# K and V tails with zero rows for the other pair of heads, in a fused attention and expert kernel

## The chip, the cores and the metric

The kernel runs on one core of one Trainium2 chip. The metric is device time in microseconds (us) of one execution; the figure for a kernel is the median of several executions. A second source of numbers is one execution that the hardware profiler recorded, instruction by instruction; its own time and span stand beside the median below.

## The reference

Three blocks follow each other: a linear attention with a norm per head, a feed-forward block with squared ReLU, and a mixture of four experts. Only the first is touched.

```python
def _attn_ref(q, k, v, g_norm):          # 4 batches, 8 heads, 576 positions, 64 wide
    kv = np.einsum('bhsd,bhse->bhde', k, v)
    out = np.einsum('bhsd,bhde->bhse', q, kv)
    rms = np.sqrt(np.mean(out * out, axis=-1, keepdims=True) + 1e-06)
    return out / rms * g_norm
def _moe_ref(x, w_in, w_out):            # 2304 tokens, 512 -> 2048 -> 512
    h = np.maximum(x @ w_in, 0.0)
    return h * h @ w_out
def _moe2_ref(x, domain_probs, w1, w2):  # 4 experts, 512 -> 1024 -> 512, weighted by probs
    ...
```

## The kernel before

**Attention.** Two heads are put side by side, so that a pair is 128 columns wide; there are 4 batches with 4 pairs each, 16 pairs in all. For pair i, `att_kv(i)` (lines 451 to 462) sums K-transposed times V over the 576 positions into one PSUM tile `pk`: four matmuls over 128 positions each (line 457, operands `kvs` or `kvm`), and one over the last 64 positions, the tail (line 458, operand `kvt`). The two diagonal 64x64 blocks of `pk` are copied to `kvd`, one by ScalarE (line 460) and one by VectorE (line 461). `att_out(t)` multiplies a tile of 128 positions of q with four of the `kvd` blocks (line 472, into `po`); ScalarE squares it (line 481), VectorE sums the squares (line 482). `att_c` makes the norm's factor for a group of tiles on VectorE and writes the normed tile `xn` (line 504). `att_b` transposes `xn` on TensorE (line 515, into `pt`), and ScalarE and GpSimd split the result into a high and a low part `x` (lines 213 and 214). All of attention is done in float32, and the trace shows two records for each such matmul.

**The tail.** `kvt[b]` holds the tails of a batch's four pairs on 128 partitions: pairs 0 and 2 on partitions 0 to 63, pairs 1 and 3 on partitions 64 to 127. The tail matmul of a pair reads its 64 partitions only; the trace gives its shape as 64x128, that of line 457 as 128x128.

**Order.** `RAMP` is a list of units (k: `att_kv`, o: `att_out`, c: `att_c`, b: `att_b`, w and y: narrowing and splitting of weights, f and g: first and second matmul of the feed-forward block). The units of the ramp go through a scheduler that sets the order of each engine's instructions from its own estimates of their times; only the second stage, the experts, is in an order written out by hand. Every engine runs its own instructions in order and waits for others by semaphores. Nearly all loads go through the queue of SyncE (SP), also in order. `load_kv(i + 8)` is called at the end of `att_kv(i)` (line 462), `load_q(t + 4)` in `att_out(t)` (line 479). The tiles `kvm` (pairs 6 to 15) and `kvt` have two buffers, `q` has four, so that a load may have to wait until TensorE has read what lay there: the load of `kvm9` waits for the line 457 matmuls of pair 7.

**After attention**, TensorE runs the matmuls of the feed-forward block (lines 550, 564, 723) and of the experts (lines 845 and 909) until the end. Their weights come in as `raw` (line 234), are narrowed by ScalarE and VectorE (lines 240 to 257) and split by ScalarE and GpSimd (lines 394 to 396).

Of the kernel before, what the change touches and what calls it, by code (L numbers as in the profile page):

```python
# [10 lines left out]
F32 = mybir.dt.float32  # L11
# [7 lines left out]
P = 128  # L19
B, H, S, D = 4, 8, 576, 64  # L20
# [3 lines left out]
STAIL = S - NCK * P  # L24
# [158 lines left out]
def fused_kernel(ctx, tc, kvm, kvt, qt, g2, probs, probs_t, w64, w32, out, out_t):  # L183
    nc = tc.nc
# [241 lines left out]
    kv_in, q_in, tails, stage, st_t, po_t, att_mid = {}, {}, {}, [None], {}, {}, {}  # L426
    NSTAGE = 6

    def load_kv(i):
        if i >= B * NPAIR:  # L430
            return
        b, c = divmod(i, NPAIR)
        if i < NSTAGE:
            if i % 2 == 0:
                stage[0] = accp.tile([P, 2, 2, NCK, P], F32, tag=f"acc{i // 2 + 1}", name=f"kvs{i}")
            m = stage[0][:, i % 2]
        else:
            m = attp.tile([P, 2, NCK, P], F32, tag="kvm", name=f"kvm{i}")
        nc.sync.dma_start(out=m, in_=kvm[b, c])
        if c == 0:  # L440
            tails[b] = attp.tile([P, 2, 2, P], F32, tag="kvt", name=f"kvt{b}")
            nc.sync.dma_start(out=tails[b], in_=kvt[b])
        kv_in[i] = m

# [6 lines left out]
    def att_kv(i):  # L451
        m = kv_in.pop(i)
        b, c = divmod(i, NPAIR)
        tl = tails[b][c % 2 * STAIL : (c % 2 + 1) * STAIL, c // 2]
        pk = ps.tile([P, 512], F32, tag="ps", name=f"pk{i}")
        for n in range(NCK):
            nc.tensor.matmul(pk[:, :P], m[:, 0, n, :], m[:, 1, n, :], start=(n == 0), stop=False)  # L457
        nc.tensor.matmul(pk[:, :P], tl[:, 0, :], tl[:, 1, :], start=False, stop=True)
        kd = kvd[i % NKVD]
        nc.scalar.activation(out=kd[:D, :D], in_=pk[:D, :D], func=AF.Copy)  # L460
        nc.vector.tensor_copy(kd[D:, D:], pk[D:, D : 2 * D])
        load_kv(i + NSTAGE + 2)
# [472 lines left out]
    def probs_keep():  # L935
# [10 lines left out]

    unit = dict(
        k=att_kv, o=att_a, c=att_c, b=att_b, w=split_w, y=split_narrowed, p=probs_p, n=probs_keep, f=g1, g=g2a, x=right, e=right_first, l=half_load, s=g1s, h=g2b, q=g2q, r=second_right, u=prepare, d=move
    )
    ext = early = None  # L950
# [4 lines left out]
    with ExitStack() as actx:  # L955
        attp = actx.enter_context(tc.tile_pool(name="attp", bufs=2))
# [12 lines left out]
        for _ in range(2):  # L969
            nc.tensor.matmul(idle, zero[:, :P], zero, start=True, stop=True)  # L970
        nc.scalar.activation(out=warm, in_=warm, func=AF.Sqrt)
        load_kv(0)
        load_kv(1)
        load_w(0)
        load_kv(2)
# [69 lines left out]
```

## Time and profile before

| | us |
|---|---|
| median of 3 runs | 1157.28 (1157.25 to 1157.65) |
| the profiled execution, its time | 1157.0 |
| the profiled execution, its span | 1155.1 |
| TensorE busy (share of the span) | 1138.3 (99%) |
| VectorE, GpSimd, ScalarE busy | 927.6, 786.3, 514.8 |
| tail matmuls on TensorE | 16 instructions, 32 records |

The span runs from the first to the last instruction, and the execution's time lies 1.9 us above it. Of the views, two matter most here. The chain of waits follows the work that ended last back from the last instruction; each of its rows is a start, a length and what filled it, so that consecutive records of one kind show TensorE's pace. The timeline lists the instructions of an engine in order of time, with the idle time before each and what ended it.

### The profile page before, as it was taken

Reading aid. Unit: us, or ns where it says so; the run is one execution under the profiler, and the core shown is the slowest. Engines: PE = TensorE matmul, PEld = TensorE weight load, DVE = VectorE, ACT = ScalarE, POOL = GpSimd, SP = SyncE. Lnnn points to the kernel's source line nnn. Section 1 sums busy time; section 2 is a strip of 40 time slices with the busy share of each in tenths; the row PEclk is TensorE's granted clock in tenths of the full one; section 3 lists DMA queues with packets and bytes.
Section 4 is the critical chain, followed back from the end, with each engine's and each line's share of the span. In section 5 each row is a group of like instructions: output and inputs, shape, how many; then the busy total and the mean of one; then the engine's idle time right before and its main releaser. Section 6 shows DMA issues by size and latency. Waiting matters only on the chain.

```text
span 1155.1 us, 15647 instructions
## 1 busy us (share of the span) xinstructions
PE 1138.3 (99%) x5514; PEld 953.2 (83%) x5514; DVE 927.6 (80%) x1471; ACT 514.8 (45%) x897; POOL 786.3 (68%) x675
## 2 busy tenths in 40 slices
PE   8999999999999999999999999999999999999998
PEld 6878888888888887888888888888778888888886
DVE  6866789788676667888888888888978888888888
ACT  4575545555444564644445444445543221212121
POOL 2566666656464666888888888878876565656565
PEclk9999999999999999999999999999999999999999
DMA  8811130855464535888778888875665646565652
GB/s 310 283 46 55 56 146 19 310 179 206 146 214 160 191 92 186 309 256 276 247 246 283 265 255 255 264 264 139 162 193 190 256 160 264 167 247 194 235 184 89
DMA packets 62549, 231.03 MB, mean 200 GB/s; under 512 B 6115, under 2 KB 20195, under 8 KB 46215
## 3 DMA queue, kind: packets, MB, share of 16 engines
q1 hardware_dynamic: 56278, 210.20, 50.2%
q0 software_dynamic: 5760, 19.66, 9.1%
q8 instruction: 44, 0.72, 0.2%
q14 instruction: 35, 0.28, 0.1%
q10 hardware_dynamic: 432, 0.17, 0.1%
HBM read 138.49 MB, written 71.86 MB: 182 GB/s over the span
## 4 chain that ended last, share of the span: by engine, by line
PE 93%; POOL 2%; DMA 2%; ACT 1%; DVE 1%; issue 1%; SPq 0%; DVEq 0%; POOLq 0%; ACTq 0%
PE p L564 17%; PE p L550 10%; PE pc L723 10%; PE pa L723 10%; PE pd L723 10%; PE qc L845 7%; PE qd L845 7%; PE qa L845 7%; PE pb L723 5%; PE qb L845 4%; PE p L909 4%; PE po L472 1%; DMA kvs<-in_kvm 1%; PE pk L457 1%; DMA raw<-in_w 1%; DMA b<-hb 1%
## 5 line engine op out<-in xcount | busy, mean ns | idle before, releaser
L564 PE MATMUL p<-hh,b 128*128 128x512 f32 (+1 forms) x640 | 193.8, 369 | 0.0
L214 POOL TENSOR_TENSOR hl<-r,hh 128x512 fp32r<-128x512 f32 (+1 forms) x80 | 98.4, 1242 | 91.3 <-ACT hh L213 91.2
L564 PEld LDWEIGHTS p<-hh,b 128*128 128x128 f32 x640 | 116.8, 189 | 20.2 <-ACT hh L213 0.2
L214 POOL TENSOR_TENSOR b<-hb,b 128x512 fp32r<-128x512 f32 x62 | 81.1, 1309 | 69.9 <-ACT b L213 69.8
L571 DVE TENSOR_TENSOR acc<-p,acc 128x512 f32<-128x512 f32 (+1 forms) x140 | 87.7, 634 | 40.8 <-PE p L564 39.6
L564 PE MATMUL p<-hl,b 128*128 128x512 f32 (+1 forms) x320 | 118.3, 370 | 0.8 <-POOL hl L214 0.8
L213 ACT ACTIVATE b<-hb 128x512 fp32r<-128x512 f32 x62 | 38.9, 627 | 169.4 <-PE qa L845 159.9
L214 POOL TENSOR_TENSOR a<-w,a 128x512 fp32r<-128x512 f32 x44 | 62.2, 1419 | 56.7 <-ACT a L213 56.7
L723 PE MATMUL pa<-o,a 128*128 128x512 f32 x384 | 98.1, 391 | 2.2 <-ACT p L734 2.2
L723 PE MATMUL pc<-o,a 128*128 128x512 f32 x384 | 97.6, 389 | 0.8 <-DVE u L738 0.8
L723 PE MATMUL pd<-o,a 128*128 128x512 f32 x384 | 97.7, 390 | 0.1
L723 PEld LDWEIGHTS pc<-o,a 128*128 128x128 f32 x384 | 72.0, 188 | 16.2 <-DVE u L738 1.3
L723 PEld LDWEIGHTS pa<-o,a 128*128 128x128 f32 x384 | 71.0, 188 | 17.0 <-ACT p L734 3.1
L723 PEld LDWEIGHTS pd<-o,a 128*128 128x128 f32 x384 | 71.9, 188 | 15.6 <-DVE pb L743 0.8
L550 PE MATMUL p<-x,a 128*128 128x512 f32 (+1 forms) x432 | 83.8, 344 | 0.1
L550 PEld LDWEIGHTS p<-x,a 128*128 128x128 f32 x432 | 69.4, 189 | 11.0 <-POOL x L214 0.6
L564 PEld LDWEIGHTS p<-hl,b 128*128 128x128 f32 x320 | 60.4, 189 | 11.5 <-POOL hl L214 1.6
L867 DVE TENSOR_TENSOR acct<-qc,acct 128x512 f32<-128x512 f32 x90 | 61.8, 686 | 2.5 <-POOL acct L875 2.1
L867 DVE TENSOR_TENSOR acct<-qa,acct 128x512 f32<-128x512 f32 x90 | 61.5, 685 | 0.2 <-PE qa L845 0.2
L845 PE MATMUL qd<-t4b,b 128*128 128x512 f32 x192 | 54.5, 391 | 1.3 <-DVE acct_r L867 0.8
L214 POOL TENSOR_TENSOR t<-t1f,t 128x512 fp32r<-128x512 f32 x31 | 45.4, 1463 | 14.1 <-ACT t L213 14.1
L845 PE MATMUL qa<-t4b,b 128*128 128x512 f32 x192 | 54.1, 390 | 0.6 <-POOL t4b L214 0.6
(230 smaller groups left out, 2952.4 us busy)
## 6 DMA issues: line engine op xcount, KB each, us to landing
raw<-in_w SPq DMA_DIRECT2D x64, 512.0 KB, 4.6
a_kept<-a SPq DMA_DIRECT2D x28, 1024.0 KB, 4.8
a<-a_kept SPq DMA_DIRECT2D x28, 1024.0 KB, 10.2
t<-th_kept_t SPq DMA_DIRECT2D x27, 1024.0 KB, 6.9
b_kept<-b SPq DMA_DIRECT2D x14, 1024.0 KB, 6.2
bs<-bs_kept SPq DMA_DIRECT2D x14, 1024.0 KB, 7.3
b<-raw POOLq DMA_DIRECT2D x16, 512.0 KB, 5.1
bs_kept<-o SPq DMA_DIRECT2D x7, 1024.0 KB, 4.3
```

The lines of the kernel that those rows point to most:

```text
L213: nc.scalar.activation(out=hi, in_=full, func=AF.Copy)
L214: engine.tensor_tensor(out=lo, in0=full, in1=hi.bitcast(F32), op=ALU.subtract)
L457: nc.tensor.matmul(pk[:, :P], m[:, 0, n, :], m[:, 1, n, :], start=(n == 0), stop=False)
L472: nc.tensor.matmul(po[done : done + n, c * P : (c + 1) * P], q[:, c, done : done + n], kvd[(b * NPAIR + c) % NKVD], start=True, stop=True,)
L550: nc.tensor.matmul(pt[:, :n], w, x, start=(i == 0), stop=(i == len(steps) - 1))
L564: nc.tensor.matmul(pt[:, :n], w, h, start=(i == 0), stop=(i == len(steps) - 1))
L571: nc.vector.tensor_tensor(out=a, in0=pt[:, :n], in1=a, op=ALU.add)
L723: nc.tensor.matmul(pr[bank], x, y, start=(m == 0 and not more), stop=(m == len(steps) - 1), skip_group_check=more,)
L845: nc.tensor.matmul(pt, x, y, start=(m == 0 and not more), stop=(m == len(steps) - 1), skip_group_check=more)
L867: nc.vector.tensor_tensor(out=to, in0=pt, in1=to, op=ALU.add)
L909: nc.tensor.matmul(pt, h, w, start=(i == 0), stop=(i == len(steps) - 1))
```

## The change

The host lays the tails out anew. For each pair of neighbours (0 and 1, 2 and 3) the tile has three blocks of 128 columns on 128 partitions: K of the even pair with zeros on partitions 64 to 127, V of both, K of the odd pair with zeros on partitions 0 to 63. The tail matmul now takes all 128 partitions, with K from the first or the third block and V from the second; the zeros cancel the other pair's rows. The load of a batch's tails grows from 256 KB to 384 KB.

```diff
         if c == 0:
-            tails[b] = attp.tile([P, 2, 2, P], F32, tag="kvt", name=f"kvt{b}")
+            tails[b] = attp.tile([P, 2, 3, P], F32, tag="kvt", name=f"kvt{b}")
             nc.sync.dma_start(out=tails[b], in_=kvt[b])
...
-        tl = tails[b][c % 2 * STAIL : (c % 2 + 1) * STAIL, c // 2]
+        tl = tails[b][:, c // 2]
...
-        nc.tensor.matmul(pk[:, :P], tl[:, 0, :], tl[:, 1, :], start=False, stop=True)
+        nc.tensor.matmul(pk[:, :P], tl[:, c % 2 * 2, :], tl[:, 1, :], start=False, stop=True)
...
-    kvt = kvt.reshape(B, P, 2, 2, P)
+    kt, vt = kvt.reshape(B, 2, STAIL, 2, 2, P).transpose(4, 0, 1, 2, 3, 5)
+    kvt = np.zeros((B, 2, STAIL, 2, 3, P), np.float32)
+    kvt[:, 0, :, :, 0], kvt[:, 1, :, :, 2], kvt[:, :, :, :, 1] = kt[:, 0], kt[:, 1], vt
+    kvt = kvt.reshape(B, P, 2, 3, P)
```

The number of instructions is the same on every engine. Because the scheduler of the ramp sees a larger load and another shape of matmul, it also puts some instructions in another order. On SP's queue, in the stretch that loads for pairs 8 to 11 (`kvm8` to `kvm11`, `kvt3`) and for the tiles 4 to 7 of q:

```order
 L234 DMA raw0_2_176<-in_w64 128x512
 L439 DMA kvm8_162<-in_kvm 128x1024
+L439 DMA kvm9_186<-in_kvm 128x1024
 L449 DMA q4_214<-in_qt 128x512
-L439 DMA kvm9_186<-in_kvm 128x1024
 L449 DMA q5_224<-in_qt 128x512
-L442 DMA kvt3_252<-in_kvt 128x512
+L442 DMA kvt3_252<-in_kvt 128x768
 L449 DMA q6_260<-in_qt 128x512
-L439 DMA kvm10_196<-in_kvm 128x1024
 L449 DMA q7_270<-in_qt 128x512
-L439 DMA kvm11_206<-in_kvm 128x1024
```

The load of `kvm9` now stands ahead of that of `q4` instead of behind it; `kvm10` and `kvm11` move back behind `q7`, the load of `raw0_3` and `q8`.

On TensorE, around the tail of pair 4 (`pk4`) and the q tile 2 (`po2`):

```order
 L457 MATMUL pk4_242<-kvs4_145 128x128 x4
-L458 MATMUL pk4_242<-kvt1_147 128x128
 L472 MATMUL po2_255<-kvd0_96,q2_140 128x128
 L472 MATMUL po2_255<-kvd1_97,q2_140 128x128
+L458 MATMUL pk4_242<-kvt1_147 128x128
 L472 MATMUL po2_255<-kvd2_98,q2_140 128x128
 L472 MATMUL po2_255<-kvd3_99,q2_140 128x128
```

The tail of pair 4 moves two instructions back; the rest of TensorE's order is as it was. On VectorE the sum of squares of tile 6 moves four instructions back, behind the norm's factor for tiles 4 and 5, and the first step for `raw0_3` one forward; on ScalarE the square of tile 6 moves behind one small instruction; GpSimd's order is unchanged.

## Rows read from the trace of the kernel before

**Rows 1.** The page, part 4: shares of the chain that ended last.

```profile
PE 93%; POOL 2%; DMA 2%; ACT 1%; DVE 1%; issue 1%; SPq 0%; DVEq 0%; POOLq 0%; ACTq 0%
```

**Rows 2.** The chain of waits, 2 to 31 us: start, length in us, what.

```profile
2.12 6.60 DMA raw<-in_w
...
8.74 7.81 DMA kvs<-in_kvm
...
16.69 1.13 PE pk L457 x8
...
18.23 2.00 PE po L472 x16
...
25.11 0.91 PE pk L457 x8
...
26.03 0.33 SPq L439
...
26.41 3.88 DMA q<-in_qt
```

**Rows 3.** The chain of waits, 32 to 71 us.

```profile
32.39 0.41 PE pk L458 x2
32.80 1.09 PE po L472 x8
33.89 2.76 PE p L550 x12
...
37.54 0.42 PE pk L458 x2
37.95 2.97 PE p L550 x12
...
53.55 0.91 PE po L472 x8
...
56.45 2.52 POOL x L214 x2
...
66.33 0.59 PE pt L515 x4
...
70.41 0.44 PE pt L515 x4
```

**Rows 4.** Line 458: engine, operation, xcount: duration in ns min/median/max, starts, forms.

```profile
L458 PE MATMUL pk<-kvt x32: 272/322/374, 6.3 to 66.1; 64*128 64x128 f32 x32
```

**Rows 5.** Loads issued at 23.4, then of 0 to 75 us: KB, us to landing.

```profile
q<-in_qt SPq DMA_DIRECT2D x1, 256.0 KB, 3.7
...
kvm<-in_kvm SPq DMA_DIRECT2D x10, 512.0 KB, 5.0
```

**Rows 6.** Timeline of TensorE, 26 to 31 us: start, length, engine, line, [idle before].

```profile
26.35 0.66 PE L515 MATMUL pt<-ident,xn 128*128 128x128 f32 x4
...
27.13 1.34 PEld L472 LDWEIGHTS po<-kvd,q 128*64 128x64 f32 x16 [0.36 <-DMA q<-in_qt]
28.64 0.97 PEld L457 LDWEIGHTS pk<-kvm 128*128 128x128 f32 x8 [0.17 <-PE po L472]
```

**Rows 7.** Timeline of ScalarE and of weight loads, 65 to 68 us.

```profile
66.23 0.60 ACT L892 ACTIVATE r<-p 128x512 f32<-128x512 f32 x1 [0.67 <-POOL a L396]
...
66.85 1.23 PEld L472 LDWEIGHTS po<-kvd,q 128*64 128x64 f32 x15 [0.17 <-ACT r L892]
```

**Rows 8.** Stretches: busy (x) of PE, PEld, DVE, ACT, POOL; clock, DMA share, GB/s.

```profile
10.00:20.00 10.00, 8.40 (x62) 7.51 (x63) 6.77 (x18) 3.19 (x8) 2.54 (x2) 1.00 1.04 402
50.00:60.00 10.00, 9.86 (x63) 8.47 (x62) 9.63 (x21) 6.59 (x14) 4.59 (x4) 1.00 0.47 159
1151.40:1155.10 3.70, 0.00 (x0) 0.00 (x0) 0.76 (x2) 0.00 (x0) 0.00 (x0) 1.00 0.58 204
```

**Rows 9.** Timeline of TensorE, the first matmuls, before any data has landed.

```profile
1.46 3.78 PE L970 MATMUL idle<-zero 128*128 128x512 f32 x4 [1.46 <-DVE warm L967]
```

**Rows 10.** Timeline of VectorE, the normed tiles 4 and 5.

```profile
36.20 1.29 DVE L504 TENSOR_TENSOR xn<-po,st 128x512 f32<-128x512 f32 x2
```

## The prediction

> **What bounds the kernel now.** I read the shares of the chain first: TensorE holds 93% of it [rows 1]. After the ramp the program is one long run of matmuls, so what counts of this change is how much earlier or later TensorE gets through the ramp, the first 70 us; the order of all engines behind it is the same. Next I read the chain through the ramp [rows 2, 3], to see which of the 16 tail matmuls lie on it. To 16.69 us it is loads: `raw0_0`, and then the load of `kvs4` that SP issues only when that has landed. Then come the pair 4 matmuls, ScalarE and VectorE work on the q tiles 2 and 3, a transpose and the pair 7 matmuls at 25.11. At 26.03 SP issues the load of `kvm9`, whose buffer these have freed, and at 26.41 that of `q5`, which lands 3.88 us later. From then to 54.5 the chain is TensorE alone. A short piece on ScalarE and GpSimd follows, to 59 us, and TensorE again.
>
> **What a tail costs, and what is saved.** Groups of 128-row records run at 0.11 us a record (0.91 us for 8) [rows 2, 3]. The two records of a tail, the only ones with 64 rows [rows 4], take 0.41 us on the chain instead of 0.22: 0.19 too much. The group behind a tail is slow too: 1.09 us for 8 records of line 472 against 0.91, 2.97 for 12 of line 550 against 2.76, 0.59 for 4 transposes against 0.44 [rows 3], so 0.15 to 0.21 more. Going to 64 rows and back thus costs 0.34 to 0.40 us a tail; I take 0.39, since most groups behind a tail are of the first two kinds. With 128 rows a tail is two more records like those ahead of it, so I expect all of this to go. Sixteen times 0.39 is 6.2 us, the most that there is to gain.
>
> A rule speaks against that. The Trainium skill ("TensorE: Matmul & The Clock Gate", Part 3, "The mechanism" and what overlaps) says that a weight load overlaps matmuls in flight only where the row groups differ; a full-height tail would then lose its overlap. The trace disagrees: eight full-height loads behind each other take 0.97 us [rows 6], one each 0.12 us, with matmuls running. I go by the row, and keep the rule's case as a small rival.
>
> **Which tails lie on the path.** Pairs 0 to 3 come before 16.69 us, where loads bound everything: nothing. Pair 4 is on the chain: 0.39. Pairs 5 to 7: the chain there runs over ScalarE, VectorE, a transpose and the line 457 matmuls of pair 7, and no tail is on it: nothing. Pair 8 is followed by a wait for q5. Pairs 9 to 13, five tails, lie in TensorE's own stretch: 5 x 0.39 = 1.95. Pair 14 ends just ahead of the first-layer matmuls that wait for GpSimd's split of x (at 56.45) [rows 3]: nothing. Behind pair 15 TensorE waits 0.17 us for ScalarE's `r`, and this for GpSimd's `a` [rows 7], so I count nothing there either.
>
> **The larger loads.** Each batch brings 128 KB more. In the load-bound start the queues move 402 GB/s [rows 8], so that is 0.33 us. `kvt0` is ahead of `raw0_0`, and so of `kvs4`: 0.33 later. `kvt1`, `kvt2` and `kvt3` are issued behind the load that the chain waits for next. With pair 4's tail this leaves 0.06 us gained when the q tiles 2 and 3 are done, and that the tail has moved between matmuls of `po2` alters nothing, as all of these run without a pause.
>
> **The loads that change places.** This is the larger term. In the kernel before, `q4` was issued at 23.4, ahead of `kvm9`, and landed 3.7 us later [rows 5]; TensorE had waited 0.36 us for it when it began `po4` at 27.13 [rows 6]. Now `kvm9` stands ahead of it, and SP cannot issue that before the line 457 matmuls of pair 7 are done, at 26.03 - 0.06 = 25.97. All behind it on SP's queue waits too: q4, q5, `kvt3`, q6, q7. `q4` takes the place that `q5` had, is issued at 26.35 and lands 3.88 us later, at 30.23; `po4` starts at 30.28, 3.15 late. From there TensorE has to do what it had done before by 30.14: `po4`, 1.51 us (27.13 to 28.64, the starts in [rows 6]), and pair 8, 10 records at 0.11 and 0.1 more at the first, behind `po4`'s narrow tiles (half of what a tail costs), 1.22. So `po5` starts at 33.01 and not at 30.34 (behind its 0.05 from the landing of q5), and as it no longer follows a pause its first record is 0.10 shorter: TensorE is 2.57 us late.
>
> Less 1.95 for the five tails, that is **0.62 us late** where the chain leaves TensorE at 54.5. The piece on ScalarE and GpSimd starts from the end of `po12` and moves with it, and so does all that follows.
>
> What must be late for nobody: `kvm10` now waits behind `q8`, which needs q4's buffer and so `po4`'s end (31.9), and for pair 8 (32.95). At 5.0 us [rows 5] it lands at 38.0; TensorE wants it at 38.65. `kvm13`, which waits for pair 11, has 0.2 us in hand by the same reckoning; a load slower by 0.5 us would add 0.3. VectorE's work on tiles 4 and 5 slips with `po4`: the normed tiles [rows 10] come some 2.0 us later, at 38.2 to 39.5, and the buffer of the first is wanted by TensorE at about 39.8.
>
> **Sum.** `po4` starts 3.15 late, `po5` 2.67 and, by its first record, 2.57; less 1.95; together +0.6. The profiled execution of 1157.0 becomes 1157.6, its span 1155.7; the median is 0.28 above that execution, so 1157.28 becomes **1157.9**. About 0.2% (2.3 us: 1155.0 to 1159.6) is what a measurement of this kernel can tell from no change.
>
> **Rivals.**
> *The late q4 costs nothing*, because it lands sooner than q5 did, or other work is late there anyway: then five tails and 0.06 stay, -2.0, or -2.8 with the tails of pairs 14 and 15. 1154.5 to 1155.3. For it: a single q load issued at 23.4 took 3.7 us and not 3.88 [rows 5], so some of the landing time is the neighbours'. Against it: SP issues in order, and the order is known.
> *The clock falls.* Between the transposes of tile 2 (end at about 26.6) and `po4` TensorE now stands still for 3.6 us, where it had waited 0.36 [rows 6]. At the start it runs at the lower of its two levels, 1.2 GHz: four records of 512 columns took 3.78 us [rows 9], 0.95 each, where 4 x 0.11 is the pace of later ones. If the wait brings it down, and it needs as long to rise as there, half of 3.8 us is lost: +0.6 + 1.9, 1159.8, or 1161.7 for two such stretches. Against it: at the end the granted clock is still 1.00 over 3.7 us without a matmul [rows 8]. It decides if this pause, in the thin work around it, brings the clock down. The Trainium skill (same page, Part 1) has the clock fall when the engine idles; the trace shows no fall inside the program. This case is slower than before.
> *VectorE's lag reaches the path.* It is busy for 9.63 of the 10 us from 50 to 60 [rows 8], and if the delay of 1.8 us with which it enters that stretch (2.57 less two tails, taken over from the first-layer matmuls) is not made up by 62, it passes over GpSimd's `a` and ScalarE's `r` [rows 7] to TensorE at 66.85: +1.8 instead of +0.6, 1159.1, at most 1160.
> *The tail keeps its cost* (the rule above, or the delay comes from something other than the rows): the late loads stand alone, +2.6 to +3.0, 1159.9 to 1160.3.
>
> **How the numbers follow.** Forecast 0.60 (1157.2 to 1158.9); q4 costs nothing 0.14, of it 0.06 beyond 0.2%; clock 0.10, all slower; lag 0.12, 0.05 of it slower; tail keeps its cost 0.04, slower. So faster 0.06, same 0.75, slower 0.19. The range from 1155.3 to 1159.9 leaves out about half of the first rival and most of the clock case, under 2 in 10.
>
> **What would show it.** Line 458 at 0.27 us a record with 0.11 between starts, as line 457; SP's issue of q4 behind that of `kvm9`; TensorE idle for over 3 us ahead of `po4` at 30.3, waiting for q; `po5` at 33.0; granted clock 1.00 throughout; from 70 us on all starts shifted by the same 0.6 us. I am wrong if `po4` starts before 29, if TensorE waits for `kvm10`, `kvm13` or for VectorE between 33 and 54, or if the records behind the wait are twice as long.

## The result, and the profile after

The changed kernel takes 1164.21 us (median of four executions, 1161.57 to 1164.37) against 1157.33 (1157.25 to 1157.65): a ratio of 1.0051, with an interval of 1.0040 to 1.0063. It is slower by 6.9 us, and the prediction of 1157.9, with a range to 1159.9, was wrong. One execution of a later run, e7, took 1908 us at a granted clock of 0.56 and is in no number below; it is also that run's only trace, so that e7 is read by its times alone. The profiled execution took 1164.35 with a span of 1162.6, 7.5 above that of before. TensorE's share of the chain went from 93% [rows 1] to 92%, VectorE's from 1% to 2%. The page of after, part 4:

```profile
PE 92%; DVE 2%; POOL 2%; DMA 2%; ACT 1%; issue 1%; SPq 0%; DVEq 0%; POOLq 0%; ACTq 0%
```

**The tails did what was expected.** The view of line 458 gives 275 ns where it had given 322 in the median [rows 4], and on the chain a tail takes 0.22 us where it took 0.41 [rows 3] (38.26 in the second fence below):

```profile
L458 PE MATMUL pk<-kvt x32: 275/275/421, 7.2 to 69.7; 128*128 128x128 f32 x32
```

**Four delays ate far more.** First the start. The chain of waits of after (start, length in us, what) begins with the same two loads as before [rows 2]:

```profile
2.13 7.55 DMA raw<-in_w
...
9.70 7.81 DMA kvs<-in_kvm
...
17.64 1.13 PE pk L457 x8
```

`raw0_0`, behind the larger `kvt0`, lands after 7.55 us instead of 6.60, and pair 4 starts 0.95 later. Then come the loads that changed places, as forecast:

```profile
25.67 0.89 PE pk L457 x8
26.56 0.24 PE pk L458 x2
26.80 0.12 SPq L439
...
26.97 3.84 DMA q<-in_qt
...
30.86 2.88 PE po L472 x16
33.74 2.01 PE pk L457 x8
35.74 0.43 PE pk L458 x2
...
38.26 0.22 PE pk L458 x2
38.48 0.89 PE po L472 x8
```

SP issues `kvm9` when pair 7 is done, then `q4`, which lands 3.84 us later. `po4` starts at 30.86 instead of 27.13. But look at the lengths right behind it: 2.88 us for the 16 records of `po4`, 2.01 for 8 records of 128 rows, 0.43 for a tail. All are about twice what they take at the full clock. The stretches of after (busy time of each engine, then TensorE's granted clock, DMA share, GB/s) say why:

```profile
26.00:28.00 2.00, 1.22 (x12) 0.98 (x10) 1.86 (x3) 1.57 (x4) 1.41 (x2) 1.00 0.46 55
28.00:30.00 2.00, 0.00 (x0) 0.00 (x0) 1.90 (x5) 1.18 (x3) 2.00 (x2) 0.96 0.80 316
30.00:32.00 2.00, 1.14 (x7) 1.15 (x9) 0.32 (x1) 0.00 (x0) 2.00 (x3) 0.50 1.01 352
32.00:34.00 2.00, 2.00 (x13) 1.67 (x11) 0.00 (x0) 0.23 (x1) 0.59 (x1) 0.50 1.05 411
34.00:36.00 2.00, 2.00 (x11) 2.00 (x11) 1.56 (x3) 0.92 (x2) 0.00 (x0) 0.50 0.74 252
36.00:38.00 2.00, 2.00 (x17) 2.00 (x17) 1.33 (x3) 1.27 (x3) 0.98 (x1) 0.83 0.48 156
...
60.00:66.00 6.00, 5.68 (x34) 4.46 (x33) 5.90 (x13) 3.46 (x8) 3.52 (x3) 1.00 0.08 28
...
72.00:74.00 2.00, 0.33 (x2) 0.19 (x2) 0.23 (x1) 1.97 (x5) 2.00 (x2) 1.00 0.40 158
74.00:76.00 2.00, 2.00 (x11) 1.97 (x11) 0.69 (x1) 1.49 (x3) 2.00 (x3) 0.56 0.41 89
76.00:78.00 2.00, 2.00 (x13) 2.00 (x13) 1.00 (x3) 0.99 (x3) 0.87 (x1) 0.59 0.11 42
```

TensorE stands still for 3.6 us from 27.2, and its clock is at the lower level (0.50, 1.2 GHz) from 29.9 to 36.7. It falls a second time, from 74.2 to 77.7, again with a pause just ahead. The timeline of TensorE shows that pause inside `po13`, and the chain shows what it waits for:

```profile
70.39 1.36 PE L472 MATMUL po<-kvd,q 128*64 128x128 f32 x14
73.67 3.99 PE L472 MATMUL po<-kvd,q 128*64 128x128 f32 x18 [1.92 <-DVE kvd L461]
```

```profile
67.84 0.61 DVE u L251
...
68.47 0.70 DVE m L254
...
69.33 1.29 POOL u L395
...
70.69 1.28 POOL a L396
...
71.99 0.61 ACT r L892
...
72.62 0.63 ACT r L893
73.25 0.12 ACT kvd L460
...
73.39 0.24 DVE kvd L461
```

Pair 15's block (the tile `kvd7`) is copied by ScalarE behind the two steps of `r`, and `r` waits for GpSimd's `a`, which comes of VectorE's narrowing of a weight. In the kernel before there was no such stop: the record of `po13` that reads `kvd7` began at 68.05, and `kvd7` was ready 0.19 us ahead of it, at 67.86. VectorE's timeline of before:

```profile
67.63 0.23 DVE L461 COPY kvd<-pk 64x64 f32<-64x64 f32 x1 [3.81 <-ACT kvd L460]
```

The chain of after runs mostly over VectorE from 47.3 to 69.2, and VectorE is busy for 5.90 of the 6 us from 60 to 66. Part of this is, by the rows, waiting and not work. Between 51 and 66 us four small operations of the norm (lines 496 and 500, 16 or 24 columns) take 0.92 to 1.16 us each instead of 0.17, each beside an operation of GpSimd that ends with it, and all four lie on the chain. The kernel before has two such operations in its stretch, with 1.3 us above 0.17 each, against 3.6 in after. One of the four, and GpSimd's operation beside it:

```profile
65.20 1.10 DVE L500 TENSOR_TENSOR st<-st 128x16 f32<-128x16 f32 x1
```

```profile
64.99 1.28 POOL L214 TENSOR_TENSOR x<-xg,x 128x512 fp32r<-128x512 f32 x1 [2.11 <-ACT x L213]
```

The start of the same group in both profiles gives the account:

| group | before | after | later by |
|---|---|---|---|
| pair 4 | 16.69 | 17.64 | 0.95 |
| `po4` | 27.13 | 30.86 | 3.73 |
| `po5` | 30.34 | 35.96 | 5.62 |
| pair 9 | 31.33 | 37.20 | 5.87 |
| `po12` | 53.39 | 57.29 | 3.90 |
| `po13` | 66.85 | 70.39 | 3.54 |
| the transposes behind `po13` (`pt10`) | 70.25 | 77.45 | 7.20 |
| matmuls of line 564 at 120 us | 120.39 | 127.64 | 7.25 |

Between pair 9 and `po12` TensorE wins back 1.97 us by its tails. It loses 3.66 in `po13`: the record that reads `kvd7` begins 3.28 us after the first instead of 1.20, which is 2.08, and the rest, at the lower clock, takes 1.58 longer. From there on almost nothing changes.

### The profile page after: what moved, and what is told of

The parts are those of the page before. It is cut to its first block, busy times and chain, and to the rows that moved or that the text cites. A ratio compares the mean times of both kernels' runs of the same rounds, so it can differ in the third digit from the quotient of the medians.

```text
span 1162.6 us, 15648 instructions
## 1 busy us (share of the span) xinstructions
PE 1138.4 (98%) x5514; PEld 955.8 (82%) x5514; DVE 930.4 (80%) x1471; ACT 515.4 (44%) x897; POOL 787.1 (68%) x675
## 4 chain that ended last, share of the span: by engine, by line
PE 92%; DVE 2%; POOL 2%; DMA 2%; ACT 1%; issue 1%; SPq 0%; DVEq 0%; POOLq 0%; ACTq 0%
PE p L564 16%; PE p L550 10%; PE pa L723 10%; PE pc L723 10%; PE pd L723 10%; PE qc L845 7%; PE qd L845 7%; PE qa L845 7%; PE pb L723 5%; PE p L909 4%; PE qb L845 4%; PE po L472 1%; DMA kvs<-in_kvm 1%; DMA raw<-in_w 1%; PE pk L457 1%
```

## The experiments

In most of them the order of the loads is held by dependencies that carry no wait (NoSync), in the list of before or that of after:

```diff
+        line = "m7 t2 w2 m8 q4 m9 q5 t3 q6 ...".split()   # before; after: "... m8 m9 q4 q5 t3 q6 ..."
+        for first, then in zip(line, line[1:]):
+            tc.add_manual_dep(dma[then], dma[first].name, ...)
```

The kernel before ran along each time: 1157.10, 1157.53 and 1157.10 us (medians of 21, 28 and 27 executions of three jobs).

**Three parts apart: e1, e2, e3.** e1 has the full tails and larger loads in the old places. e2 is the kernel before with the loads in the new places. e3 has the larger loads in the old places, and the tail reads its 64 rows:

```diff
-        tl = tails[b][:, c // 2]
+        tl = tails[b][c % 2 * STAIL : (c % 2 + 1) * STAIL, c // 2]
```

> The changed kernel with the loads on SP pinned to the order of the kernel before (q4 ahead of kvm9, kvm10 and kvm11 ahead of q7, raw0_3 and q8); tails on 128 rows, 384 KB loads. Theory A (the order makes a pause ahead of po4, and the pause costs the clock): no pause over 0.5 us at po4, granted clock 1.00 from 17 us on, pair 4's tail saves 0.39 and pairs 9 to 13 save 1.95, the larger loads take back 0.33 to 0.95: 1155.3 to 1156.0 where the kernel before has 1157.3. Theory B (the larger loads are what costs): the order changes little, 1160 or more.

> The kernel before, tails on 64 rows and 256 KB loads, with the loads on SP pinned to the order of the changed kernel. Theory A: TensorE pauses for about 3.2 us ahead of po4, the granted clock falls to 0.50 for some 7 us, and without the tails' 2 us this is slower than the changed kernel: 1164 to 1167; if the clock stays up, 1160. Theory B: 1157.3, as the loads are small.

> The kernel before with tail loads of 384 KB (three blocks), its tail matmuls still on 64 partitions, the order of all loads as before. Theory A: pair 4 starts 0.33 to 0.95 later and nothing else: 1157.6 to 1158.3, clock 1.00. Theory B: 1162 to 1164, as the changed kernel.

Measured: e1 1157.88 (ratio 1.0011, 1.0002 to 1.0020), e2 1162.37 (1.0048, 1.0033 to 1.0064), e3 1160.06 (1.0026, 1.0015 to 1.0037). The new order of the loads alone brings most of the loss, 5.3 us, without any change of a tail; put back, it leaves 0.8 us. None of the three medians lies where theory A had it: e1 is above 1156.0, e2 below 1164, as its clock was down for about half of the 7 us, and e3 lies between the two theories. The stretches of e2 show the same fall, once; its `po13` does not stop, and TensorE stays 4.6 us late from `po5` on:

```profile
28.00:30.00 2.00, 0.00 (x0) 0.00 (x0) 1.77 (x3) 0.87 (x2) 2.00 (x3) 1.00 0.92 351
30.00:32.00 2.00, 1.64 (x14) 1.64 (x15) 0.00 (x0) 0.00 (x0) 2.00 (x2) 0.74 1.00 331
32.00:34.00 2.00, 2.00 (x10) 1.67 (x9) 0.59 (x1) 1.15 (x2) 0.26 (x1) 0.50 1.03 398
```

e3 pays for the loads and has nothing from the tails: pair 4 starts 0.87 late in its profile, and 1158.15 is the median of its five executions with a mean granted clock of 0.999 or more. The other five (0.993 to 0.996) took 1161.3 to 1162.8.

e1 leaves a question. Its TensorE is 0.34 ahead of before at `po13`, and 0.73 behind at `pt10`. Its `po13`, too, now stops for `kvd7`, for 0.86 us:

```profile
68.73 2.41 PE L472 MATMUL po<-kvd,q 128*64 128x128 f32 x18 [0.86 <-DVE kvd L461]
```

**The clock apart from the wait: e4 and e10.** e4 is the changed kernel with its order held and spare matmuls in the first pause, written where `po4` writes later. e10 puts eight more into the second one:

```diff
+        for _ in range(15 * (t == 4)):
+            tc.keep_in_program_order(nc.tensor.matmul(po[:, :P], ident, ident, start=True, stop=True))
...
             for c in range(NPAIR):
+                for _ in range(8 * ((t, b, c) == (13, 3, 3))):      # e10 only
+                    nc.tensor.matmul(po[done : done + n, c * P : (c + 1) * P], ident[:, :n], ident, start=True, stop=True)
```

> The changed kernel, the order of every engine pinned to its own, with 15 matmuls of 128x128 on the identity ahead of po4, 3.35 us in the pause, whose result po4 overwrites. The late q4 stays, the pause is filled. Theory A: granted clock 1.00 through the ramp, po4 at 30.9 as in the changed kernel, po5 at 33.6 and not at 36.0, TensorE 1.2 us late at 54 us: 1158.5, up to 1159.5 if VectorE's lag reaches TensorE. If the clock had no part in it, and the late loads and VectorE's work cost the time: 1162 to 1164.

> The kernel of e4 (changed kernel, every order held, 15 spare matmuls in the pause ahead of po4) with 8 spare 64x128 matmuls, 1.8 us, in the second pause too, within po13 ahead of its last block. Nothing else. Theory 'clock': no stretch at half clock is left between 26 and 80, pt10 starts at 72.4 to 73.0 instead of 74.56 (the wait for kvd7 stays), and the time falls from 1162.6 to 1159.0 to 1160.0 with a spread under 1.5 us. Rival 'work, not clock': the spare matmuls only delay, pt10 is at 74.5 or later and the time stays above 1161.5.

Measured: e4 1162.64 (1160.85 to 1163.33), e10 1161.37 (1161.13 to 1162.56). In e4's profile the first fall is gone; `po4` takes 1.51 us from its start to the next group's, not 2.80, and TensorE is 0.58 late at `po13`: the forecast's 0.62. Then `po13` stops and the clock falls there, which theory A did not have, so that the time lies in the range of the case against it, 1162 to 1164. Nor did the filled pause keep the clock up throughout: of the four executions two have a mean clock of 0.998, as the profiled one, and two of 0.994, the value of after's profile; where it was down in those no trace shows. In e10 the stop is as long, but filled, and the 18 records behind it take 2.41 instead of 4.01. Timelines of TensorE, e4 and then e10 (lines moved by 4 and 6):

```profile
30.44 1.58 PE L476 MATMUL po<-kvd,q 128*64 128x128 f32 x16 [0.25 <-DMA q<-in_qt]
...
70.71 4.01 PE L476 MATMUL po<-kvd,q 128*64 128x128 f32 x18 [1.92 <-DVE kvd L463]
```

```profile
69.27 1.91 PE L477 MATMUL po<-ident 128*64 128x128 f32 x16
71.35 2.41 PE L478 MATMUL po<-kvd,q 128*64 128x128 f32 x18 [0.17 <-DVE kvd L463]
```

So the second fall costs 1.6 us, shown by the pair. The time of e10 is 1.4 above the expectation's upper end: `pt10` came at 73.60, not 72.4 to 73.0, since `kvd7` was 0.6 later than in e4, and in both kernels with spare matmuls TensorE lost another 0.8 us at 464 us, far behind the change (this I did not follow up).

**The price of the load, and where e1's gain went: e5, e6, e7, e8.** e5 is the kernel before with `tl = tails[b][:, c // 2]`; e6 is e1 with one dependency:

```diff
+        tc.add_manual_dep(dma["r0_1_1"], dma["kvd15"].name, ...)   # ScalarE: pair 15's copy, then r0_1_1
```

e7 is both, and e8 has that dependency in the changed kernel.

> The kernel before with one edit: the tail matmul reads all 128 partitions of the old 256 KB tile, so that the tails of two pairs are summed and the output is not the reference's; every load is in the place it had before. Against the earlier run with full tails, 384 KB and the old order it takes 128 KB from each batch's load and nothing else. Theory 'load': the 0.76 to 0.95 us by which pair 4 came late there is the price of the larger first load: pair 4 starts at 16.7, po4 at 27.1, po13 at 65.0 (66.85 less five tails of 0.39), and the time falls to about 1156.5 to 1157.0. Theory 'chain': TensorE's lead over the kernel before is given back at po13, which waits for kvd7, whose time is set by ScalarE and GpSimd and not by TensorE: po13 stops for over 1 us, pt10 starts at 70.0 to 70.5 as in the kernel before, and the time is 1157.0 to 1157.5.

> Full tails, 384 KB loads, every load in the place it had before, and one dependency more: ScalarE copies pair 15's block (kvd7) ahead of r0_1_1 instead of behind its two steps. Theory 'chain': po13's stop of 0.86 us goes, pt10 starts at about 70.1 instead of 70.98, and the time falls from 1157.9 by 0.8, to 1157.0. Rival 'next wait': r0_1_1 and what GpSimd makes of it come 0.2 us later, VectorE's next work sets the end, and the time stays at 1157.7 to 1158.2.

> The two edits before this one together (256 KB loads with the tails of two pairs summed, not the reference's output; kvd7 ahead of r0_1_1). Theory 'load' and theory 'chain' both right: the five tails reach the end, pt10 at about 68.3 to 68.8 and 1155.3 to 1156.0, all that was to be had. Rival 'next wait': VectorE, behind its own work of this stretch, holds the next group, pt10 starts no earlier than 69.8, and the time is above 1156.7.

> The changed kernel with its own order of the loads, and kvd7 ahead of r0_1_1 on ScalarE. The first pause, of 3.6 us ahead of po4, and the clock's fall behind it stay. Theory 'second pause': po13 does not stop for 1.92 us, the clock does not fall at 74, pt10 starts at 73.8 to 74.2 instead of 77.46, and the time is 1160.4 to 1161.0. Rival: the clock falls at 74 for another reason than this pause, or the wait moves to the next block: 1162.5 to 1164.3.

e5: 1158.09 (1156.68 to 1158.94), ratio 1.0000 (0.9991 to 1.0009). In its profile, 1156.68, the clock is up from 5.6 us to the last matmul, and pair 4 starts at 16.71, 0.74 sooner than in e1, with `raw0_0` landing as before:

```profile
2.12 6.62 DMA raw<-in_w
```

That is the load's price: 0.74 to 0.95. Theory "load" then asked for 65.0 at `po13`, and it was 65.37, 1.48 ahead of before. But the gain goes no further. Timeline of TensorE in e5:

```profile
65.37 1.36 PE L472 MATMUL po<-kvd,q 128*64 128x128 f32 x14
67.62 2.41 PE L472 MATMUL po<-kvd,q 128*64 128x128 f32 x18 [0.89 <-DVE kvd L461]
```

`kvd7` came at 67.34, in the kernel before at 67.63: 0.29 sooner, while TensorE was 1.48 sooner. `pt10` is 0.38 ahead of before, and that is all that the tails give. Theory "chain" has the right mechanism, though the stop is 0.89 and not over 1, and the median lies 0.6 above its range. Where the gain went can be read one step further back. VectorE had kept up: it begins line 501, the last step of a norm's factor, at 59.14 in e5 and at 60.28 in the kernel before, 1.14 sooner. But there this operation takes 1.31 us instead of 0.17, beside GpSimd's `x` (both are shown in the last section), and the next one, line 504, starts at 60.49 against 60.48. In e1 it takes 1.30.

e6: 1158.55 (1.0007, 0.9998 to 1.0016), no better than e1. In its profile, the slowest of its executions, with a fall at 17.95, the stop in `po13` is gone, but TensorE stood still 4.5 us behind the start of `pt10`, first for VectorE's `xn` and then for GpSimd's `x`:

```profile
76.51 0.47 PE L550 MATMUL p<-x,a 128*128 128x512 f32 x1 [1.25 <-DVE xn L504]
77.53 1.65 PE L550 MATMUL p<-x,a 128*128 128x512 f32 x6 [0.55 <-POOL x L214]
```

e7: 1157.16 (0.9993, 0.9984 to 1.0002), at best 1156.5. The rows of e6 show its rival "next wait", with a time 0.35 above the range; for e7 the median speaks for that rival, and no trace shows the wait.

e8: 1163.46 (1160.20 to 1164.62), 2.5 us above what theory "second pause" allowed and within its rival's range. Its profile shows e6's reason: the stop moved on, and from `pt10` to the transposes 12 us later TensorE went from 0.6 to 3.1 us behind the kernel before. Its profiled execution, the fastest of five at 1160.20, shows something else. It has the long pause, and no fall behind it:

```profile
30.51 1.58 PE L472 MATMUL po<-kvd,q 128*64 128x128 f32 x16 [3.50 <-DMA q<-in_qt]
```

The other four took 1162.8 to 1164.6, with a mean clock of 0.996 to 0.997 instead of 0.999, which fits a fall behind the pause in them, though no trace of them shows where it was. Of the three traces with such a pause left empty (after, e2, e8), two show the fall and one does not.

**Who holds the gain: e9, e11, e12.** e9 is e5 with two of VectorE's operations for `raw1_0` cut down; e11 is e1, e12 the kernel before, each with four copies moved to ScalarE:

```diff
-            out=bits, in0=high, scalar=0xC0000000, in1=bits, ...
+            out=bits[:, :few], in0=high[:, :few], scalar=0xC0000000, in1=bits[:, :few], ...   # e9, few = 16 for raw1_0; line 254 alike
```

```diff
+            if j == 0:
+                nc.scalar.activation(out=a, in_=pt[:, :n], func=AF.Copy)                      # e11, e12
+            else:
                 nc.vector.tensor_copy(a, pt[:, :n])
```

> The kernel of e5 (tails over 128 rows, 256 KB loads, old places of the loads; the tails of two pairs are summed) with every engine's order held as it was there, and two VectorE operations of 0.67 and 0.70 us (lines 248 and 254 of raw1_0, between 57 and 63 us) cut to 16 columns, so that this weight comes out wrong too. In e5 TensorE was 1.48 ahead of the kernel before at po13, and po13 then stopped for 0.89 on a chain of VectorE, GpSimd and ScalarE to kvd7. Theory 'VectorE holds the gain': kvd7 comes over 0.9 us sooner, the stop goes, pt10 starts at 68.8 to 69.0 (1.3 to 1.5 ahead of before), and that stays to the end: 1155.6 to 1155.9. Rival 'GpSimd or a load holds it': the stop stays within 0.2 of 0.89 and the time at 1156.7 to 1158.1.

> A version meant for use: full tails, 384 KB loads, the loads in the places of the kernel before, and the four first copies of acc (line 569, 0.68 us each, 50 to 57 us) on ScalarE instead of VectorE. Theory 'VectorE holds the gain': po13 no longer stops (0.86 in e1), pt10 starts at 69.8 to 70.1 and the time is 1156.8 to 1157.1 where the clock stays up; with the larger loads that is 0.3 to 0.5 better than before at most. Rival 'ScalarE becomes late': its four further copies delay the squares and kvd blocks, pt10 stays at 70.9 or later, 1157.9 or more.

> The kernel before with its own tails and loads and the same four copies on ScalarE: the control for e11. Theory: there VectorE holds TensorE for 0.17 us only, so that nothing over 0.3 is gained: 1156.7 to 1157.3 where the clock stays up, pt10 at 70.0 to 70.3. Rival: the copies alone carry a gain of 0.5 or more, and e11 owes its time to them and not to the tails.

e9: the five executions with a clock of 0.999 took 1155.43 to 1156.2 (median 1155.77), inside the 1155.6 to 1155.9 of theory "VectorE holds the gain"; no execution of e5 came below 1156.68, none of the kernel before below 1156.67. Over all eleven it is 1156.95 (0.9995, 0.9987 to 1.0004), since in six the clock had fallen. The profile has such a fall (16.6 to 20.0), so that TensorE comes to `po13` 1.27 later than in e5 and would have stopped less anyway. Counted from `po4`, `kvd7` came after 39.7 us there, in e5 after 40.9. But two things changed at once: the two operations are 1.0 us shorter together, and line 501, which now begins 0.41 us ahead of GpSimd's `x`, takes 0.17 again instead of 1.31. So e9 shows that the gain is held on the way over VectorE to `kvd7`; how much of it by VectorE's own work and how much by its wait for GpSimd, no run tells apart.

e11: 1157.50 (1.0005, 0.9996 to 1.0014); e12: 1157.58 (1.0007, 0.9998 to 1.0016), above the 1157.3 that its theory allowed. `po13` no longer stops in e11, but its profile had a long fall from 8.2 to 15.0, and TensorE came later; `pt10` at 70.59 lies between theory and rival. In the control the copies alone cost 0.3 us (`pt10` at 70.55), on a chain over ScalarE. These two do not tell the theories apart. They do show that the obvious repair gains nothing: no version that computes the reference was faster than the kernel before.

## Why the prediction was wrong

**What a tail costs: right.** 0.22 on the chain, no slow group behind it; between pair 9 and `po12` 1.97 us came back, forecast 1.95. The rule that I had weighed against it (the Trainium skill, "TensorE: Matmul & The Clock Gate", Part 3, "The mechanism": a weight load overlaps matmuls in flight only where the row groups differ) is contradicted: these tails, each record with such a load, run at the pace of their neighbours.

**The loads that change places: right.** SP's order, the issue behind pair 7 and the wait of over 3 us came as worked out. Where the clock stayed up (e4), TensorE was 0.58 late at `po13`, forecast 0.62.

**The larger loads: mis-sized.** The term was 128 KB at 402 GB/s, 0.33. It measured 0.95 in after, and 0.74 between e1 and e5. That the load is the cause is shown; why 128 KB more in `kvt0` delay `raw0_0` by more than their share of the rate is not.

**The clock: the step that failed.** The sum has no term for it. I gave this rival 0.10 on the row in which the clock stays at 1.00 for 3.7 us at the end [rows 8], and took that for a rule. The row was a single case; it told what can happen, not what mostly does. In that trace itself the clock fell about 0.4 us behind the window, 4.1 us after the last matmul. The same stretch of after ends at the lower level:

```profile
1158.60:1162.50 3.90, 0.00 (x0) 0.00 (x0) 0.76 (x2) 0.00 (x0) 0.00 (x0) 0.64 0.56 196
```

There the last matmul ends at 1158.6 and the clock falls at 1159.7. Over the thirteen traces (e7's left out) the fall comes 1.1 to 4.1 us after the last matmul, and the kernel before is the latest of them. In eleven of them it comes within 3.6 us. Before the change I had only the one trace, and it happened to be the latest: that was bad luck. To leave the clock out of the sum on a single row was the fault. The pause ahead of `po4` brought the clock down in the profiles of after and e2, by the times probably in most executions of e8, and not in e8's profile. The rival's price for one stretch, 1.9, was near (2.4 us from `po4` to `po5` in after, with 6.8 us at half clock), and its second stretch came too, but for a reason that I had put under another rival. The Trainium skill (the same page, Part 1) has the clock fall when the engine idles; after and e2 agree, with 3.6 and 3.3 us idle ahead of a fall, and so do the rows at 74 us, with 1.9; e8's profile does not.

**VectorE's lag: the second failed step.** I treated it as one case among several, with 0.12, and counted nothing at `po13`, though a row spoke for it: VectorE busy for 9.63 of 10 us [rows 8]. The other row I misread. The gap of 0.17 ahead of `po13` [rows 7] is no wait for `r`: the same 0.17 stands between weight loads at 28.64 [rows 6], and ahead of `po13` in after and in e1, with other operations named as its end. What counted was not there: that `kvd7` was ready 0.19 us before its reader. In the busy stretch the delay was not made up: `po5` was 5.62 late, and `kvd7` 5.76. It arrived at `po13` as a stop of 1.92 where there had been none. The path was the one that I had named, over `a` and `r`, but with a last step that I had not, the copy of `kvd7` behind `r` on ScalarE. And the pause brought the clock down again, 1.6 more. On the same path the gain was lost: of 1.48 us in e5, 0.38 were left 4.5 us later. How much of the lag is VectorE's own work stays open, as its busy time holds waits for GpSimd, 2.2 us more of them in after than in before.

The sum in these terms, from the profiled execution of before: forecast +0.6; loads +0.6; first fall +2.4; stop for `kvd7` +2.1; second fall +1.6; together 7.3, measured 7.35 (smaller shifts of both signs are left out: 0.25 lost behind `po5`, where the clock was down until 36.7, and 0.36 won between `po12` and `po13`). The two cases were not alternatives. The late load fed both, and the stop of the second made a pause for the first.

## What to carry to other kernels

Before a gain on the busiest engine is summed up, look for the next stretch in which a helper is as busy as it is: there the gain can end, and a delay can go on to the end. Then see how much of the helper's busy time is work and how much a wait for a third engine, as short operations that take many times their usual time show. A change of shape that lets a scheduler reorder loads should be timed with the old order held, so that the edit and the reordering are seen apart. And a new pause of TensorE of some 3.5 us is to be priced with half clock behind it, as the likelier case here, and the chance of that is to be read from more than one trace.

## What the runs showed of the hardware

- **Shorter pauses bring the clock down too, by chance.** In the load-bound start the clock fell during or within 1 us behind pauses of 1.2 us (e1, fall at 10.9) and 2.0 us (e9 at 16.6, e6 at 17.95), for 3.4 us each. In the kernel before a pause of 1.6 us at 15.1 had no such effect. With full tails and the loads in their old places (e1, e5, e6, e7, e9, e11) such falls are more frequent: a mean clock of 0.998 or less in 37 of 66 executions, in the kernel before in 14 of 76. With the larger loads alone (e3) it is 5 of 10, so the tails are not the only way to them. Why was not tried. With it go medians that lie 0.5 to 1.5 us above the fastest execution of the same kernel.
- **A small operation of VectorE can wait for a large one of GpSimd.** Line 501, on 16 columns, takes 0.17 us at 60.28 in the kernel before, 0.15 ahead of GpSimd's `x`, and 1.31 in e5, where it starts with `x` and ends with it. Timelines of VectorE in before, of VectorE in e5 and of GpSimd in e5:

```profile
60.28 0.17 DVE L501 SCALAR_TENSOR_TENSOR st<-st 128x16 f32<-128x16 f32 x1
```

```profile
58.94 0.17 DVE L500 TENSOR_TENSOR st<-st 128x16 f32<-128x16 f32 x1
59.14 1.31 DVE L501 SCALAR_TENSOR_TENSOR st<-st 128x16 f32<-128x16 f32 x1
```

```profile
59.13 1.29 POOL L214 TENSOR_TENSOR x<-xg,x 128x512 fp32r<-128x512 f32 x1 [1.27 <-ACT x L213]
```

The Trainium skill ("GPSIMD Engine Reference", section 1, Specifications) says that GpSimd shares its interface to SBUF with VectorE. The two rows of e5 agree, and show a price in this kernel: 1.1 us on the chain that ends at `kvd7`.
